# Channel weight pieces in three transfers over 128 partitions, and another order of the decode steps of the token weight pieces

## The chip, the cores and the metric

The kernel runs on one core of one Trainium2 chip, in one launch. A core has five engines with instruction streams of their own: PE multiplies matrices, DVE (VectorE) and ACT (ScalarE) work element by element on 128 partitions, POOL (GpSimd) does small copies and starts some transfers, SP (SyncE) starts the others. Sixteen DMA queues in hardware move the data between HBM and the on-chip memory. The metric is the time of one execution in device microseconds; the lower, the better. Three runs of the kernel before gave 2074.94, 2076.41 and 2078.41 us, so the median is 2076.41.

## The reference

Eight batches of 4096 tokens with 192 values each. First a causal convolution over seven tokens with softmaxed taps, one set of taps for each of eight heads; then a mixing over the tokens, and one over the channels, each with two products, a ReLU between them and a residual.

```python
# w: softmax of weight (8 heads x 7 taps); x_unf: the 7 tokens up to each one
x = np.einsum('hk,bskhg->bshg', w, x_unf).reshape(B, S, D)
xt = x.transpose(0, 2, 1)
h = np.maximum(xt @ w_tok1, 0.0) @ w_tok2          # 4096 -> 256 -> 4096 tokens
u = x + h.transpose(0, 2, 1)
h2 = np.maximum(u @ w_ch1, 0.0) @ w_ch2            # 192 -> 1536 -> 192 channels
return (u + h2).astype(np.float32)
```

The weights come as float64. The kernel reads them as pairs of 32-bit words and makes float32 values of them on the chip ("decoding").

## The kernel before, in words

The batches are worked in five groups (one, one, two, two, two). Within a group the tokens go in tiles of 512: `mix2` adds the token mixing, `transposed` turns the result, `channel1` and `channel2` do the two products of the channel mixing. The convolution and the first token product of the next group run as background beside them. All this takes from about 67 us to the end and is not touched.

What matters here is the opening, `stage1_first`, in which the first batch is convolved on PE (`conv_mm`, with `conv_out` on ACT), the weights are loaded and decoded, and the first token product is summed up (`mix`, L423, into `ps_a`). The work is cut into twelve decode **jobs**, numbered n: jobs 0 to 7 are the eight pieces of `w_tok1` ("token weight pieces", 1024 KB each, results `t_0` to `t_7`), job 8 the first piece of `w_tok2` (1024 KB), jobs 9 to 11 the three **channel pieces** of `w_ch1` (768 KB each). Three pieces of `w_ch2` and a second piece of `w_tok2` follow.

A job goes through these steps, by line:

- L203, `load`: SP issues the transfer into a raw buffer (`dec_raw`, four of them in turn, or `early_raw` for jobs 2, 5 and 8). The issue waits until the buffer's last reader is through, which is L176 of an earlier job.
- L167 on ACT (`begin`): the absolute value, which waits for the landing.
- L169, L170, L173, L176 on DVE, in this order: clamp, shift, sign, low bits. L169 waits for L167. L173 and L176 read the raw buffer again.
- For jobs 8 to 11 also L182 on ACT and L183 on DVE (`split`): the value is split into a high and a low part, `w_hi` and `w_lo` for the channel pieces, `t2s` for `w_tok2`.

Every engine runs its instructions in the order in which they were written, so a waiting instruction holds up all behind it. The order on DVE comes from `woven`, which takes one step from each of its lists in turn: in round n the first two steps of job n, the last two of job n-1, and the split of job n-2. On ACT, L167 of job 11 stands behind the `t2s` split of job 8 and ahead of the first `w_hi` (L182, job 9) and of `h` (L352 in `mix1_done`, the result of the first token product). DVE makes the low half of `h` at L353. `mix2` of the first tile (L844 to L846 on PE) needs `h` and `t2s`, and the first channel products (L919) need `w_hi` and `w_lo`.

SP issues in the order of the program: jobs 8 to 11, the first piece of `w_ch2`, four stores of the convolved batch (`xcd`, L508), then the other two pieces of `w_ch2` and the second piece of `w_tok2`. POOL copies the second tile (`load_next`, L897) when the store of `u` to `xcd` has landed and its buffer is free, and then stores the decoded `w_tok1` (`t1d`, L415) in eight transfers.

A channel piece covers the rows 0 to 191 of `w_ch1` as three blocks c of 64 (`ND` is 3, `D2` is 64), and 256 columns of each of the two column halves h. On the chip the half h = 0 lies on partitions 0 to 63 and h = 1 on partitions 64 to 127. Before, a piece is two transfers, one for each half:

```python
ws = w_ch1.rearrange("(c p) n -> p c n", p=D2)
src = [
    (slice(h * D2, (h + 1) * D2), slice(0, ND * n), ws[:, :, 2 * (h * NP * P + cs.start):2 * (h * NP * P + cs.stop)])
    for h in range(2)
]
```

Of the kernel before, what the change touches and what calls it, by code (L numbers as in the profile page):

```python
# [114 lines left out]
def conv_mixer_kernel(ctx: ExitStack, tc: tile.TileContext, x, weight, w_tok1, w_tok2, w_ch1, w_ch2, out):  # L115
# [6 lines left out]
    P = 128  # L122
# [3 lines left out]
    D2 = P // 2  # L126
    ND = D // D2
    NP = NF // 2
# [12 lines left out]
    w_tok1, w_tok2, w_ch1, w_ch2 = (w.bitcast(U32) for w in (w_tok1, w_tok2, w_ch1, w_ch2))  # L141
# [43 lines left out]
    class Decoder:  # L185
# [5 lines left out]
        def load(self, src, shape, rows=P, raw=None):  # L191

            n = 1
            for s in shape:
                n *= s
            if raw is None:
                raw = self.pool.tile([P, self.n, 2], U32, name="dec_raw", bufs=self.rawbufs)
            flat = raw[:rows, :n]
            for ps, ns, s in (src if isinstance(src, list) else [(slice(0, rows), slice(0, n), src)]):
                d = flat[ps, ns].rearrange("p n t -> p (n t)")  # L200
                if len(s.shape) == 3:
                    d = d.rearrange("p (a b) -> p a b", b=s.shape[2])
                nc.sync.dma_start(out=d, in_=s)  # L203
            return flat, n
# [12 lines left out]
    def w1_job(ps):  # L217

        n = len(ps) * P
        cs = slice(ps.start * P, ps.stop * P)  # L220
        ws = w_ch1.rearrange("(c p) n -> p c n", p=D2)
        src = [
            (slice(h * D2, (h + 1) * D2), slice(0, ND * n), ws[:, :, 2 * (h * NP * P + cs.start):2 * (h * NP * P + cs.stop)])
            for h in range(2)
        ]
        return dict(
            src=src, shape=[ND, n], hi=w1[0][:, :, cs], lo=w1[1][:, :, cs],
            view=lambda v: v.rearrange("p (c n) -> p c n", n=n),
        )
# [30 lines left out]
    def woven(*lists):  # L260

        lists = [list(v) for v in lists]
        while any(lists):
            for v in lists:
                if v:
                    v.pop(0)()

    def decode_items(dec, jobs, loaded=False):
# [35 lines left out]
        def low(i):  # L304
# [7 lines left out]
            items.extend(jobs[i][2])  # L312

        load(0)
        load(1)
        begin(0)
        for i in range(len(jobs)):
            if i:
                high(i - 1)
            for k, c in enumerate((0.5, 0.5, 1, 1)):  # L320
                add(n * c, 500 if k == 0 else 0, lambda i=i, k=k: sts[i]["a"][k]())
                if k == 0 and i:
                    low(i - 1)
                if k == 2:
                    begin(i + 1)
            load(i + 2)
# [35 lines left out]
    def stage1_first(pe, p0, pd, late, load_u, load_next, after, thirds, hooks):  # L362
# [3 lines left out]
        quads = [range(s0, s0 + TJ) for s0 in range(0, NJ, TJ)]  # L366
# [33 lines left out]
        def x0_load(c):  # L400
            x0 = homes[c]
            x0s.append(x0)
            j0 = chunks[c].start
            if c == 0:
                nc.gpsimd.memset(x0[:, 0, :], 0.0)
                nc.sync.dma_start(out=x0[:, 1:], in_=xt[:, 0:NC])
            else:
                nc.sync.dma_start(out=x0, in_=xt[:, j0 - 1:j0 + NC])
# [18 lines left out]

        accs = mix1_accs()
        jobs = [t1_job(i) for i in range(len(quads))] + [t2_job(0, 0, TT)] + [w1_job(ps) for ps in thirds]
        nj = len(jobs)  # L430
        later = [lambda f=f: w2_job(f, NF // 3) for f in range(0, NF, NF // 3)] + [lambda: t2_job(0, TT, TT)]
# [8 lines left out]
        def next_load():  # L440
            n = len(sts)
            if n < nj:
                load(jobs[n])
            else:
                later[n - nj] = later[n - nj]()
                load(later[n - nj])
# [34 lines left out]
        def conv_mm(m):  # L481
            c, part = m // 2, m % 2
            x0 = x0s[c]
            n = NC
            for h2 in range(part * H // 4, (part + 1) * H // 4):
                ps = ps_x.tile([P, TT], F32, name="ps_x")
                convs.setdefault(m, []).append((h2, ps))
                for i in range(2):
                    h = 2 * h2 + i
                    o = ps[:, i * n * G:(i + 1) * n * G].rearrange("p (j g) -> p j g", g=G)  # L490
                    hs = slice(h * G, (h + 1) * G)
                    nc.tensor.matmul(out=o, lhsT=band[:, h], rhs=x0[:, 1:, hs], start=True, stop=False)
                    nc.tensor.matmul(out=o, lhsT=corner[:, h], rhs=x0[:, :n, hs], start=False, stop=True)

        def conv_out(m):
            c, part = m // 2, m % 2
            n = NC
            if c == len(xcs):
                xcs.append(up.tile([P, n, D], F32, name="u", bufs=2))
            xc = xcs[c]  # L500
            for h2, ps in convs[m]:
                nc.scalar.copy(
                    out=xc[:, :n, 2 * h2 * G:2 * (h2 + 1) * G].rearrange("p j (i g) -> p i j g", g=G),
                    in_=ps[:, :2 * n * G].rearrange("p (i j g) -> p i j g", i=2, g=G),
                )

        def xc_store(c):
            nc.sync.dma_start(out=xf[:, chunks[c].start:chunks[c].stop], in_=xcs[c])  # L508

        chains_a = []  # L510

        def begin(n):
            chains_a.append(dec.a(sts[n], jobs[n]["top"]() if "top" in jobs[n] else None))

        def split(n):
            jb = jobs[n]
            hi, lo = jb["make"]() if "make" in jb else (jb["hi"], jb["lo"])
            return dec.b(sts[n], hi, lo, jb.get("view", lambda v: v))
# [23 lines left out]
        for n in range(nj - 1):  # L542
            if n + 2 < nj:
                begin(n + 1)
            if n == 1:
                conv_mm(2)
            for m in behind.get(n, ()):
                conv_out(m)
            woven(
                chains_a[n][:2], chains_a[n - 1][2:] if n else [],  # L550
                split(n - 2) if n > 1 and "top" not in jobs[n - 2] else [],
            )
            if n + 2 == nj:
                begin(n + 1)
            for fn in work.get(n, ()):
                fn()
            if n not in (0, 6, 9):
                next_load()
            if n == 1:
                x0_load(3)  # L560
            if n == 8:
                for c in (3, 0, 1, 2):
                    xc_store(c)
            if n == 7:
                load_u(xcs[0])
            if n == 9:
                late()
        n = nj - 1
# [377 lines left out]
    def channel1(t):  # L946
        h = {}
        for f0 in range(0, NF, NF // 3):
            for n in ("hh", "hl"):
                part = hp.tile([P, NF // 3, TT], F32R, name=f"{n}{f0}")  # L950
                for f in range(NF // 3):
                    h[n, order[f0 + f]] = part[:, f]
        bg.tiled = True
        for p in range(NP):
            pss = channel1_mm(t, p)
            bg.fg(2040 if p else 2400, 1300)
            for f, ps in pss:
                nc.scalar.activation(out=h["hh", f], in_=ps, func=AF.Relu)  # L958
                nc.vector.scalar_tensor_tensor(  # L959
                    out=h["hl", f], in0=ps, scalar=0.0, in1=f32(h["hh", f]), op0=ALU.max, op1=ALU.subtract  # L960
                )
        bg.tiled = False
        return h
# [56 lines left out]
    def first_done():  # L1020
# [6 lines left out]

    thirds = [range(p, p + NP // 3) for p in range(0, NP, NP // 3)]
    stage1_first(
        pe, p0, pd, first_late, first_u, first_next, first_done, thirds,  # L1030
        [first_mix, first_transposed] + [lambda p=p: first_channel1([p]) for p in range(NP)],
# [78 lines left out]
    for gi, bs in enumerate(GROUPS):  # L1110
# [13 lines left out]
        for q in range(NT):  # L1124
            nxt = (gi, q + 1) if q + 1 < NT else (gi + 1, 0)
            for i, b in enumerate(bs):
# [12 lines left out]
                if ahead:  # L1139
                    h = channel1(abc[i])  # L1140
# [67 lines left out]
```

## Time and profile before

| what | value |
|---|---|
| median of three runs | 2076.41 us |
| the profiled execution's own time | 2077.34 us |
| its span in the trace | 2075.5 us |
| PE busy in the span | 2054.5 us |
| DVE busy | 1403.1 us |
| ACT busy | 760.5 us |
| mean granted clock of PE | 0.998 |
| first token mixing (L844) starts at | 58.40 us |
| first channel product (L919) starts at | 67.21 us |

Times in the trace count from the start of the span. A row of the timeline has its start, how long it took, the engine, the line and the operation, then what is written and read, and, in brackets, how long the engine stood idle before it and whose end it waited for. "SPq" is SP issuing a transfer; the transfer itself goes on after it. In the chain of waits a row "DMA ..." is a transfer from its issue to its landing. A stretch's row gives the busy time of PE, PEld (loading weights), DVE, ACT and POOL with their instructions, then the granted clock of PE as a share of the full one, the busy share of the sixteen DMA queues, and the GB/s that they moved.

### The profile page before, as it was taken

The numbers are of one execution on the slowest core, as the hardware profiler recorded it, in microseconds if no ns is written. First come the engines' busy times: TensorE is split into PE (matmuls) and PEld (weight loads), VectorE is DVE, ScalarE is ACT, GpSimd is POOL, SyncE is SP. The second block draws the span as 40 slices with busy tenths as digits, with TensorE's granted clock in tenths as the row PEclk, the third lists the DMA queues.
The fourth block names the chain that finished last, engine by engine and source line by source line (L and its number), as shares of the span: only waits on it lengthen the run. The fifth ranks groups of instructions, "written<-read, shape, count | busy, mean of one in ns | idle before, by whom it ended". The sixth has DMA issues, their size and how long they took to land.

```text
span 2075.5 us, 41299 instructions
## 1 busy us (share of the span) xinstructions
PE 2054.5 (99%) x17723; PEld 1901.4 (92%) x17723; DVE 1403.1 (68%) x2781; ACT 760.5 (37%) x1305; POOL 102.0 (5%) x167
## 2 busy tenths in 40 slices
PE   9899999999999999999999999999999999999999
PEld 9789899998988999999999999999999999999998
DVE  7899969999549989447965678444455544444444
ACT  4565534434333433223333324232232332233222
POOL 0100000000000000000000000000000000000000
PEclk9999999999999999999999999999999999999999
DMA  9745536554363555143543343322211122222210
GB/s 296 284 150 166 162 119 202 157 151 151 117 173 115 168 166 175 60 113 93 150 117 87 105 125 114 103 77 67 59 48 56 50 64 67 59 67 67 67 32 16
DMA packets 259654, 239.44 MB, mean 115 GB/s; under 512 B 202832, under 2 KB 213584, under 8 KB 257936
## 3 DMA queue, kind: packets, MB, share of 16 engines
q1 hardware_dynamic: 243616, 158.55, 26.8%
q0 software_dynamic: 15856, 78.26, 11.8%
q8 instruction: 140, 2.29, 0.4%
q14 instruction: 42, 0.34, 0.0%
HBM read 146.60 MB, written 71.30 MB: 105 GB/s over the span
## 4 chain that ended last, share of the span: by engine, by line
PE 88%; DVE 6%; DMA 3%; ACT 1%; issue 1%; SPq 1%; ACTq 0%
PE ps_x L919 35%; PE ps_x L993 16%; PE ps_x L976 16%; PE ps_x L994 7%; PE ps_x L879 2%; DVE xc L629 2%; PE ps_x L851 2%; PE ps_x L853 2%; PE ps_a L714 2%; PE ps_a L715 2%; PE ps_x L852 2%; PE ps_a L716 2%; DVE hl L959 1%; DMA dec_raw<-in_moe_w_tok_dram 1%; DMA t<-t1d 1%; PE ps_x L848 1%
## 5 line engine op out<-in xcount | busy, mean ns | idle before, releaser
L958 ACT ACTIVATE hh<-ps_x 128x512 fp32r<-128x512 f32 x756 | 411.0, 597 | 807.9 <-PE ps_x L919 807.9
L959 DVE SCALAR_TENSOR_TENSOR hl<-ps_x,hh 128x512 fp32r<-128x512 f32 x756 | 485.0, 685 | 217.6 <-ACT hh L958 216.8
L919 PE MATMUL ps_x<-own,w_hi 64*128 64x512 f32 x2880 | 606.0, 390 | 1.2 <-DVE hl L959 0.9
L993 PE MATMUL ps_x<-w,hh 128*128 128x384 f32 x1872 | 542.9, 361 | 0.2 <-DVE hl L959 0.2
L919 PEld LDWEIGHTS ps_x<-own,w_hi 64*128 64x128 f32 x2880 | 426.2, 184 | 57.8 <-issue 6.5
L994 PE MATMUL ps_x<-w,hl 128*128 128x192 f32 x1872 | 468.7, 250 | 0.0
L919 PE MATMUL ps_x<-other,w_hi 64*128 64x512 f32 x1728 | 451.0, 389 | 0.5 <-DVE osb L998 0.3
L629 DVE SCALAR_TENSOR_TENSOR xc<-raw,cw,xc 128x384 f32<-128x384 f32 (+1 forms) x768 | 388.5, 561 | 9.7 <-ACT xc L627 9.7
L994 PEld LDWEIGHTS ps_x<-w,hl 128*128 128x128 f32 x1872 | 357.5, 191 | 0.0
L993 PEld LDWEIGHTS ps_x<-w,hh 128*128 128x128 f32 x1872 | 351.5, 188 | 0.9 <-DVE hl L959 0.8
L919 PEld LDWEIGHTS ps_x<-other,w_hi 64*128 64x128 f32 x1728 | 314.0, 184 | 33.0 <-DVE hl L959 1.9
L976 PE MATMUL ps_x<-w,hh 64*128 64x384 f32 x2304 | 329.9, 355 | 0.0
L919 PE MATMUL ps_x<-own,w_lo 64*128 64x512 f32 x1440 | 325.3, 386 | 0.0
L976 PE MATMUL ps_x<-w,hl 64*128 64x192 f32 x2304 | 292.1, 247 | 0.1
L919 PE MATMUL ps_x<-other,w_lo 64*128 64x512 f32 x864 | 242.1, 386 | 0.0
L919 PEld LDWEIGHTS ps_x<-own,w_lo 64*128 64x128 f32 x1440 | 216.2, 184 | 25.4
L976 PEld LDWEIGHTS ps_x<-w,hl 64*128 64x128 f32 x2304 | 223.5, 188 | 1.7 <-DVE hl L959 0.8
L976 PEld LDWEIGHTS ps_x<-w,hh 64*128 64x128 f32 x2304 | 219.7, 184 | 0.9
L997 DVE TENSOR_TENSOR osb<-ps_x,u 128x192 f32<-128x192 f32 x156 | 55.4, 355 | 208.1 <-PE ps_x L994 208.0
L919 PEld LDWEIGHTS ps_x<-other,w_lo 64*128 64x128 f32 x864 | 159.0, 184 | 16.4
L881 ACT CAST own<-ps_x 128x512 fp32r<-128x512 f32 x120 | 63.1, 594 | 270.0 <-PE ps_x L879 270.0
L984 DVE TENSOR_TENSOR osb<-ps_x,osb 128x192 f32<-128x192 f32 x288 | 103.0, 358 | 17.4 <-DVE osb L984 0.9
(126 smaller groups left out, 1885.6 us busy)
## 6 DMA issues: line engine op xcount, KB each, us to landing
raw<-in_x_dram SPq DMA_DIRECT2D x56, 672.0 KB, 7.2
t<-t2d SPq DMA_DIRECT2D x64, 512.0 KB, 5.1
out_dram<-osb POOLq DMA_DIRECT2D x63, 384.0 KB, 4.3
u<-xcd SPq DMA_DIRECT2D x62, 384.0 KB, 5.7
xcd<-xc POOLq DMA_DIRECT2D x28, 768.0 KB, 7.1
other<-own POOLq DMA_DIRECT2D x24, 768.0 KB, 5.4
t<-t1p SPq DMA_DIRECT2D x32, 512.0 KB, 4.0
t<-t1d SPq DMA_DIRECT2D x32, 256.0 KB, 4.6
```

What stands on the lines that cost most here:

```text
L629: nc.vector.scalar_tensor_tensor(out=dst, in0=src, scalar=cw[:, h, k:k + 1], in1=dst, op0=ALU.mult, op1=ALU.add)
L714: nc.tensor.matmul(out=ps, lhsT=wh, rhs=xh, start=a, stop=False)
L715: nc.tensor.matmul(out=ps, lhsT=wh, rhs=xl, start=False, stop=False)
L881: nc.scalar.copy(out=own[:, 0, c], in_=ps)
L919: nc.tensor.matmul(out=ps, lhsT=w1[w][rows, c, p * P:(p + 1) * P], rhs=t[h][rows, v, c], start=n == 0, stop=n == len(prods) - 1,)
L958: nc.scalar.activation(out=h["hh", f], in_=ps, func=AF.Relu)
L959: nc.vector.scalar_tensor_tensor(out=h["hl", f], in0=ps, scalar=0.0, in1=f32(h["hh", f]), op0=ALU.max, op1=ALU.subtract)
L976: nc.tensor.matmul(out=ps[:, :m], lhsT=h[part, f][ks, ts], rhs=w2[ks, f, :m], start=n == 0 and part == "hh", stop=z and part == "hl",)
L984: nc.vector.tensor_tensor(out=osb[:, j], in0=v, in1=osb[:, j], op=ALU.add)
L993: nc.tensor.matmul(out=ps[:, :2 * D], lhsT=h["hh", f][:, ts], rhs=w2[:, f, :], start=n == 0, stop=False)
L994: nc.tensor.matmul(out=ps[:, :D], lhsT=h["hl", f][:, ts], rhs=w2[:, f, :D], start=False, stop=z)
L997: nc.vector.tensor_tensor(out=rows(osb[:, j]), in0=rows(ps[:, :D]), in1=tokens(u, i)[:, j], op=ALU.add)
```

## The change

It has two parts. In the first, a channel piece is loaded in three transfers, one for each block c of 64 rows, and each goes to all 128 partitions. The source of such a transfer is walked h, p, n: two halves, 64 rows in each, 512 words in each row. The destination is walked as 128 partitions with 512 words. The other loads keep their shape; the test in `load` is there so that such a three-dimensional source keeps a two-dimensional destination.

In the second, the lists that `woven` takes from are exchanged in rounds 1 to 7: the last two steps of job n-1 come ahead of the first two of job n, one by one in turn. Rounds 8 on stay as they were.

```diff
             for ps, ns, s in (src if isinstance(src, list) else [(slice(0, rows), slice(0, n), src)]):
                 d = flat[ps, ns].rearrange("p n t -> p (n t)")
-                if len(s.shape) == 3:
+                if len(s.shape) == 3 and s.shape[0] == P:
                     d = d.rearrange("p (a b) -> p a b", b=s.shape[2])
                 nc.sync.dma_start(out=d, in_=s)
...
         n = len(ps) * P
         cs = slice(ps.start * P, ps.stop * P)
-        ws = w_ch1.rearrange("(c p) n -> p c n", p=D2)
+        ws = w_ch1.rearrange("(c p) (h n) -> c h p n", p=D2, h=2)
         src = [
-            (slice(h * D2, (h + 1) * D2), slice(0, ND * n), ws[:, :, 2 * (h * NP * P + cs.start):2 * (h * NP * P + cs.stop)])
-            for h in range(2)
+            (slice(0, P), slice(c * n, (c + 1) * n), ws[c, :, :, 2 * cs.start:2 * cs.stop]) for c in range(ND)
         ]
...
+            chains = [chains_a[n][:2], chains_a[n - 1][2:] if n else []]
+
             woven(
-                chains_a[n][:2], chains_a[n - 1][2:] if n else [],
+                *(chains[::-1] if n < len(quads) else chains),
                 split(n - 2) if n > 1 and "top" not in jobs[n - 2] else [],
             )
```

On SP, from job 8 to the stores of the convolved batch, the queue of transfers was this. A row is the line, the destination and source, and the destination's walk; `x6` is six alike in a row. `in_moe_w_ch_dram` stands for both channel weights.

```order
L203 DMA early_raw<-in_moe_w_tok_dram 128x2x1024
L203 DMA dec_raw<-in_moe_w_ch_dram 64x3x512 x6
L203 DMA dec_raw<-in_moe_w_ch_dram 128x4x384
L508 DMA xcd_75<-u 128x1536
L508 DMA xcd_75<-xc_0_122 128x1536
```

And it is now (lines behind the change in `w1_job` stand one lower in the count):

```order
L203 DMA early_raw<-in_moe_w_tok_dram 128x2x1024
L203 DMA dec_raw<-in_moe_w_ch_dram 128x1x512 x9
L203 DMA dec_raw<-in_moe_w_ch_dram 128x4x384
L507 DMA xcd_75<-u 128x1536
L507 DMA xcd_75<-xc_0_122 128x1536
```

Six transfers of three blocks on 64 partitions became nine of one block on 128; what stands ahead and behind is the same. On DVE, rounds 6 and 7 and the start of round 8 (job 8 is the first `dec_top`) were:

```order
L169 TENSOR_SCALAR t_6_131<-t_6_131 128x1024
L173 SCALAR_TENSOR_TENSOR t_5_130<-early_raw,t_5_130 128x1024
L170 TENSOR_SCALAR t_6_131<-t_6_131 128x1024
L176 SCALAR_TENSOR_TENSOR t_5_130<-early_raw,t_5_130 128x1024
L169 TENSOR_SCALAR t_7_132<-t_7_132 128x1024
L173 SCALAR_TENSOR_TENSOR t_6_131<-dec_raw,t_6_131 128x1024
L170 TENSOR_SCALAR t_7_132<-t_7_132 128x1024
L176 SCALAR_TENSOR_TENSOR t_6_131<-dec_raw,t_6_131 128x1024
L169 TENSOR_SCALAR dec_top<-dec_top 128x1024
L173 SCALAR_TENSOR_TENSOR t_7_132<-dec_raw,t_7_132 128x1024
```

The same rounds now:

```order
L173 SCALAR_TENSOR_TENSOR t_5_130<-early_raw,t_5_130 128x1024
L169 TENSOR_SCALAR t_6_131<-t_6_131 128x1024
L176 SCALAR_TENSOR_TENSOR t_5_130<-early_raw,t_5_130 128x1024
L170 TENSOR_SCALAR t_6_131<-t_6_131 128x1024
L173 SCALAR_TENSOR_TENSOR t_6_131<-dec_raw,t_6_131 128x1024
L169 TENSOR_SCALAR t_7_132<-t_7_132 128x1024
L176 SCALAR_TENSOR_TENSOR t_6_131<-dec_raw,t_6_131 128x1024
L170 TENSOR_SCALAR t_7_132<-t_7_132 128x1024
L169 TENSOR_SCALAR dec_top<-dec_top 128x1024
L173 SCALAR_TENSOR_TENSOR t_7_132<-dec_raw,t_7_132 128x1024
```

L173 of a piece moved ahead of L169 of the next; from L169 of `dec_top` on, the order is the old one. PE, ACT and POOL have the same rows as before.

## The prediction

> **What bounds the kernel now.** I read the page first, for the engines' shares; then the stretches with their busy times, to find where PE stands still; then the chain that ended last, in order of time, over the opening; and last the timeline of each engine there, row by row.
>
> ```profile
> PE 2054.5 (99%) x17723; PEld 1901.4 (92%) x17723; DVE 1403.1 (68%) x2781; ACT 760.5 (37%) x1305; POOL 102.0 (5%) x167
> ```
>
> PE is busy for 2054.5 of the 2075.5 us of the span, so only some 21 us are not matmuls, and a change that leaves the matmuls as they are can save little more than that; it can cost any amount. The columns of the next view are the stretch, then each engine's busy time (with instructions), the granted clock of PE, the busy share of the DMA queues and what they moved.
>
> ```profile
> 36.00:38.00 2.00, 2.00 (x14) 2.00 (x14) 2.00 (x3) 0.54 (x2) 0.00 (x0) 1.00 1.01 393
> 38.00:40.00 2.00, 2.00 (x14) 2.00 (x13) 2.00 (x3) 0.00 (x0) 0.00 (x0) 1.00 1.08 227
> 40.00:42.00 2.00, 2.00 (x15) 2.00 (x14) 0.91 (x3) 1.14 (x1) 0.00 (x0) 1.00 1.06 200
> 56.00:58.00 2.00, 0.46 (x3) 0.16 (x1) 2.00 (x3) 1.61 (x2) 0.30 (x1) 1.00 1.04 426
> 58.00:60.80 2.80, 0.35 (x1) 0.19 (x1) 2.77 (x5) 0.85 (x4) 2.80 (x4) 1.00 1.00 417
> 60.80:65.00 4.20, 4.20 (x23) 4.20 (x23) 2.16 (x5) 1.60 (x4) 4.08 (x6) 0.60 1.03 404
> ```
>
> Two things are to be seen. PE has almost nothing to do from 56.5 to 60.8, the longest hole of the run, and works at 0.60 of its clock behind it. And the DMA queues stay fully busy when their rate drops from 393 to 200 GB/s at 38: that is where the transfers of 64 partitions begin. The chain shows what fills the hole:
>
> ```profile
> 30.66 14.81 DMA early_raw<-in_moe_w_tok_dram
> 45.47 0.02 issue
> 45.49 1.15 ACT dec_top L167
> ...
> 60.80 0.36 PE ps_x L845
> ```
>
> The token piece of `w_tok2` (job 8) lands at 45.47, ACT starts on it, and from 46.66 DVE works without a pause until the token mixing of the first tile can start on PE. The rows of ACT, DVE and POOL there (an `x2` row holds two instructions):
>
> ```profile
> 51.22 0.93 ACT L167 ACTIVATE dec_top<-dec_raw 128x768 f32<-128x768 f32 x1 [2.25 <-DMA dec_raw<-in_moe_w_ch_dram]
> 53.47 1.05 ACT L182 CAST t2s<-dec_top 128x1024 fp32r<-128x1024 f32 x1 [1.33 <-DVE dec_top L176]
> 55.95 0.95 ACT L167 ACTIVATE dec_top<-dec_raw 128x768 f32<-128x768 f32 x1 [1.43 <-DVE t2s L183]
> 57.28 0.83 ACT L182 CAST w_hi<-dec_top 128x768 fp32r<-128x768 f32 x1 [0.39 <-DVE dec_top L176]
> 58.02 0.55 ACT L352 ACTIVATE h<-ps_a 128x192 fp32r<-128x192 f32 x2
> 58.15 1.47 DVE L183 TENSOR_TENSOR w_lo<-dec_top,w_hi 128x768 fp32r<-128x768 f32 x1
> 59.54 0.94 DVE L176 SCALAR_TENSOR_TENSOR dec_top<-dec_raw,dec_top 128x768 uint32<-128x768 uint32 x1
> 60.41 0.61 DVE L353 SCALAR_TENSOR_TENSOR h<-ps_a,h 128x192 fp32r<-128x192 f32 x2
> 61.38 0.96 DVE L183 TENSOR_TENSOR w_lo<-dec_top,w_hi 128x768 fp32r<-128x768 f32 x1 [0.36 <-ACT w_hi L182]
> 57.70 1.11 POOL L897 COPY u<-xc 128x768 f32<-128x768 f32 x1 [31.41 <-DMA xcd<-u]
> 58.76 6.12 POOL L415 DMA_DIRECT2D t1d<-t  x8
> ```
>
> The place to remember is ACT at 55.95: that is the Abs of the *third* channel piece. It stands in ACT's order ahead of the first `w_hi` and of `h` (L352), without which L844 to L846 cannot run. Now it waits for DVE alone, since its data are there.
>
> **The change, part one: the loads.** These are the issues in the window 0 to 110 us, with their sizes, and SP's row of the seven that begin with the channel pieces.
>
> ```profile
> 33.22 17.45 SPq L203 DMA_DIRECT2D dec_raw<-in_moe_w_ch_dram  x7
> dec_raw<-in_moe_w_ch_dram SPq DMA_DIRECT2D x6, 384.0 KB, 13.2
> dec_raw<-in_moe_w_ch_dram SPq DMA_DIRECT2D x3, 768.0 KB, 14.1
> t1d<-t POOLq DMA_DIRECT2D x8, 512.0 KB, 11.2
> xcd<-xc SPq DMA_DIRECT2D x3, 768.0 KB, 10.7
> xcd<-u SPq DMA_DIRECT2D x1, 768.0 KB, 6.8
> ```
>
> Six transfers of 384 KB (2304 KB, 2.36 MB) become nine of 256 KB, the same bytes in the same runs of 2 KB. What changes is the walk. Before, both sides of a transfer count 64 partitions outermost. Now the destination counts 128, but the source, `c h p n`, counts *two* halves h outermost and 64 rows inside. No transfer before has such a pair, so its rate must be bounded. From above by the walk with 128 on both sides: 393 GB/s, 6.0 us for all nine. Below that lies the walk of 64 on both sides, 200 GB/s with every queue busy: fewer outer steps cost rate though no queue was idle. From below by a walk whose two outer steps are all that can be dealt out: two of the 16 queues. One queue's rate is 393 / 16 = 24.6 GB/s, with 426 / 16 = 26.6 as the fastest row, so two give 49.1 (53.3), and 2.36 MB take 48.0 us (44.3). I take the low end: a share must be the same bytes on both sides, the two outer counts are 2 and 128, and cutting each along its own outer loop into equal shares works in two, the destination's halves of 64 being just the two h. In all rows seen the outer counts of both sides were equal and multiples of 16, so nothing there speaks for a finer cut.
>
> On such a transfer the Trainium skill has a rule, in "DMA: Bandwidth & Descriptors", section "Why a DMA increments its semaphore by 16 and not by 1": the number of engines is the largest up to 16 that divides the size of the slowest dimension that isn't 1 on both sides. By it 2 and 128 give two engines, hence the same sum; no run so far shows it for a count under 64.
>
> The queues pass from job 8 to the channel pieces at 38 to 39 (227 GB/s lies between 393 and 200). From 38.5 the two queues need 16.0 us for a piece: landings at 54.5, 70.5 and **86.5**. SP issues within the 17 us from 33.22 now; its waits there are for buffers that jobs 3, 4 and 6 leave by 44.77, so the queues, not SP, set these landings. What follows the third landing: Abs 0.95, w_hi 0.83, w_lo 0.96 (the 1.47 ran beside POOL's copy, which will not be there), L176 of the second piece 0.94, the first L353 and PE's start 60.80 - 60.41 = 0.39, and four hand-overs of some 0.03: 4.2 us. All else that DVE did from 50 on is done by then, in the waits for pieces one and two. L845 so starts at 90.7 in place of 60.80: **+29.9 us**, in which PE stands still.
>
> What is late next: everything behind these transfers on the same two queues. They hold a sixteenth each of three `w2` loads, four `xcd` stores, eight `t1d` stores and the second `w_tok2` piece of 1024 KB: 3 x 768 + 4 x 768 + 8 x 512 + 1024 = 10496 KB, 656 KB a queue, 25.3 to 27.3 us. That piece lands at 111.8 to 113.8. Before:
>
> ```profile
> 81.73 1.18 ACT L167 ACTIVATE dec_top<-dec_raw 128x1024 f32<-128x1024 f32 x1
> ...
> 89.28 0.36 PE L849 MATMUL ps_x<-h,t2s 128*128 128x192 f32 x1 [0.74 <-DVE t2s L183]
> ```
>
> 81.73 + 29.9 = 111.6 would leave all as it was; PE already waited 0.74 us at the end of that chain, so a delay there counts in full. It is 0.2 to 2.2; I take **+1.2**. The hole grows from 4 to some 32 us; the half clock behind it (0.60 over 4.2 us) is there already and costs about 1.7 us. I add nothing, with a second such stretch, 1.7, as the upper bound and 0 as the lower.
>
> **Part two: the order on DVE.** For jobs 1 to 7 the last two steps of the job ahead (L173, L176) now lead, so that L173 runs while L169 of the next waits for its data. Two such waits show what it may bring:
>
> ```profile
> 40.04 1.14 ACT L167 ACTIVATE t<-dec_raw 128x1024 f32<-128x1024 f32 x1 [3.50 <-DMA dec_raw<-in_moe_w_tok_dram]
> 41.21 0.69 DVE L169 TENSOR_SCALAR t<-t 128x1024 f32<-128x1024 f32 x1 [1.09 <-ACT t L167]
> 41.82 1.22 DVE L173 SCALAR_TENSOR_TENSOR t<-dec_raw,t 128x1024 uint32<-128x1024 uint32 x1
> 43.55 1.22 DVE L176 SCALAR_TENSOR_TENSOR t<-dec_raw,t 128x1024 uint32<-128x1024 uint32 x1
> 46.66 0.69 DVE L169 TENSOR_SCALAR dec_top<-dec_top 128x1024 f32<-128x1024 f32 x1 [1.89 <-ACT dec_top L167]
> ```
>
> In the wait of 1.09 the step of 1.22 finds room, so DVE is through with job 6 1.09 earlier, at 43.7 instead of 44.77. But the next step is L169 of job 8, whose place does not change, and it waits for a landing. What is won is waited for again there or, with part one as forecast, at the first channel piece until 54.5. Each of the seven L173 now stands directly behind the L170 it needs and loses the overlap that neighbours have (L173 starts 0.61 after L169, which takes 0.69): about 0.1 us each with the hand-over, 0.7 in all, inside DMA waits. I put part two at **0**, between -1.1 and +0.7.
>
> **Sum.** 29.9 + 1.2 + 0 = +31.1 us on the profiled execution's own 2077.34, that is 2108.4. That execution stands 0.9 above the median of the runs shown, 2076.41, so against the median 2107.5; I forecast **2107.5**.
>
> **The rivals.** *The load fills all queues.* If the nine go at 393 GB/s, the half rate is gone: job 8 then lands 2.7 us (1024 KB at 393) behind job 7, whose Abs started on landing at 40.04, so at 42.7; Abs ends at 43.9, and L169 of job 8 starts there (DVE free at 43.7, here part two counts) instead of 46.66: -2.8 us, 2073.6. If the hole on PE, then 1.5 us, no longer brings the half clock, 1.7 more: 2071.9. For it speaks the drop from 393 to 200 with the halves, against it the count of two. The decisive point is whether the nine take less than about 12 us.
>
> The Trainium skill, in "SBUF — State Buffer", section "Door 1: The DMA port swizzle", has it that partitions 0 to 63 reach only 8 of 16 ports and all 128 reach 16; the 393 and 200 agree with it. By it alone this rival would hold.
>
> *The shares are cut along the 64 inner rows.* Then every queue works, but on one half at a time: 200 GB/s, 11.8 us, job 8 lands as now, and the change does not do what it says: 2076.4, within a microsecond. *One queue takes each transfer whole:* 2.36 MB at 24.6 GB/s are 96 us, the third piece lands at 134, 2155.
>
> **How the numbers follow.** Two queues 0.85, all queues 0.08, no change 0.05, one queue 0.02; the first leads because two is the only count that both outer loops allow. Low end: 26.6 GB/s a queue from 38.2, nothing lost behind it: 38.2 + 44.3 + 4.2 - 60.8 = +25.9, 2102. High end: the slowest queue's landing of job 8, 45.47, on one of the two: 45.5 + 48.0 + 4.2 - 60.8 = +36.9, and 2.2 and 1.7 more, +40.8, 2117. Range 2102 to 2118, which holds nearly all of the first case. A difference of 0.2% (4 us) is what a measurement can tell from none. Faster: all queues with the clock, 0.03. Same: the rest of that rival and no change, 0.10. Slower 0.87.
>
> **What would show it.** ACT's L167 on the second and third channel piece waits for the channel DMA some 15 us each time; PE has a hole from 56.5 to about 90; the DMA rate between 46 and 80 is near 50 GB/s with a busy share near 2/16; `xcd` lands after 87. Wrong is the step of two queues if the rate at 38 to 45 stays at 200 or above, and the step behind it if L844 starts before the third piece has landed.

## The result and the profile after

| what | before | after |
|---|---|---|
| median of six runs each, same chip | 2075.55 us (2071.88 to 2078.41) | 2109.34 us (2108.77 to 2110.93) |
| the profiled execution's own time | 2077.34 us | 2109.85 us |
| its span | 2075.5 us | 2108.0 us |
| second product of the first token mixing (L845, now L846) | 60.80 us | 90.95 us |
| second half of the token mixing (L849, now L850) | 89.28 us | 121.19 us |

The ratio is 1.0164, with a 95% interval of 1.0151 to 1.0177: 33.8 us slower, in the forecast range. Lines between the two parts of the change count one lower now, those behind it one higher.

The shares of the engines, and then the stretches, in the same columns as before:

```profile
PE 2058.4 (98%) x17723; PEld 1902.7 (90%) x17723; DVE 1403.9 (67%) x2781; ACT 760.7 (36%) x1305; POOL 101.0 (5%) x167
```

```profile
38.00:40.00 2.00, 2.00 (x14) 2.00 (x13) 1.97 (x3) 1.17 (x1) 0.00 (x0) 1.00 0.29 110
46.00:56.00 10.00, 9.52 (x59) 9.22 (x57) 0.66 (x2) 0.90 (x1) 0.00 (x0) 1.00 0.14 51
60.00:70.00 10.00, 0.00 (x0) 0.00 (x0) 0.00 (x0) 0.00 (x0) 0.00 (x0) 0.51 0.13 49
80.00:88.00 8.00, 0.00 (x0) 0.00 (x0) 0.00 (x0) 0.84 (x2) 0.00 (x0) 0.50 1.04 397
96.00:100.00 4.00, 3.80 (x17) 2.83 (x18) 2.99 (x6) 2.11 (x4) 2.07 (x3) 0.50 1.02 332
```

PE's work is the same (2058.4 us against 2054.5), and what it does not work has grown from 21 to 50 us. From 40 to 77 us the queues are busy for 0.13 to 0.14 of their time, a little over two sixteenths, and move some 50 GB/s; before, the same bytes kept all of them busy at 200. From 60 to 70 no engine does anything at all. The timeline's rows of ACT and PE show who waits for what:

```profile
54.40 0.90 ACT L167 ACTIVATE dec_top<-dec_raw 128x768 f32<-128x768 f32 x1 [8.77 <-DMA dec_raw<-in_moe_w_ch_dram]
70.50 0.89 ACT L167 ACTIVATE dec_top<-dec_raw 128x768 f32<-128x768 f32 x1 [15.19 <-DMA dec_raw<-in_moe_w_ch_dram]
87.16 0.89 ACT L167 ACTIVATE dec_top<-dec_raw 128x768 f32<-128x768 f32 x1 [14.84 <-DMA dec_raw<-in_moe_w_ch_dram]
89.05 0.53 PE L845 MATMUL ps_x<-h,t2s 128*128 128x192 f32 x1 [33.53 <-ACT h L351]
90.95 0.53 PE L846 MATMUL ps_x<-h,t2s 128*128 128x192 f32 x1 [1.37 <-DVE h L352]
121.19 0.36 PE L850 MATMUL ps_x<-h,t2s 128*128 128x192 f32 x1 [0.38 <-DVE t2s L183]
```

Three pieces, three landings, some 16 us apart; behind the third the old chain runs off as it did before, and PE, which had stood still for 33.5 us, goes on. The chain of waits passes through the same place; the issues of channel transfers on SP, the last DMA piece and what follows it:

```profile
50.97 5.22 SPq L203
...
56.30 5.16 SPq L203
...
61.50 5.22 SPq L203
...
66.77 20.29 DMA dec_raw<-in_moe_w_ch_dram
...
87.16 0.89 ACT dec_top L167
88.05 0.73 ACT w_hi L182
...
88.80 0.96 DVE w_lo L183
89.76 0.87 DVE dec_top L176
90.63 0.28 DVE h L352
...
90.95 0.53 PE ps_x L846
```

SP's rows show something that the forecast did not have: each of these issues takes some 5.2 us, the ten issues that begin with the channel pieces take it 45.87 us (7 took 17.45 before), so the first store of `xcd` is issued only at 77.32.

```profile
31.35 45.87 SPq L203 DMA_DIRECT2D dec_raw<-in_moe_w_ch_dram  x10
77.32 1.06 SPq L507 DMA_DIRECT2D xcd<-u  x1
```

### The profile page after: what moved, and what is told of

Same layout as the page of the kernel before. It is cut to its first block, busy times and chain, and to the rows that moved or that the text cites. A ratio compares the mean times of both kernels' runs of the same rounds, so it can differ in the third digit from the quotient of the medians.

```text
span 2108.0 us, 41307 instructions
## 1 busy us (share of the span) xinstructions
PE 2058.4 (98%) x17723; PEld 1902.7 (90%) x17723; DVE 1403.9 (67%) x2781; ACT 760.7 (36%) x1305; POOL 101.0 (5%) x167
## 3 DMA queue, kind: packets, MB, share of 16 engines
q8 instruction: 140, 2.29, 0.4%
## 4 chain that ended last, share of the span: by engine, by line
PE 90%; DVE 4%; DMA 2%; SPq 1%; ACT 1%; issue 0%; ACTq 0%
PE ps_x L920 36%; PE ps_x L994 16%; PE ps_x L977 15%; PE ps_x L995 7%; PE ps_x L880 2%; PE ps_x L852 2%; PE ps_a L715 2%; PE ps_a L716 2%; PE ps_a L717 2%; PE ps_x L854 2%; PE ps_x L853 2%; DVE xc L630 2%; SPq L203 1%; PE ps_x L849 1%; DMA dec_raw<-in_moe_w_ch_dram 1%; DVE hl L960 1%
```

## The experiments

The kernel before ran beside each of them. Its runs spread over some 7 us (2072.48 to 2079.74). Some of that arises in the opening: in the four profiles below that share the old loads on SP and the new order, Abs of job 8 starts anywhere from 42.31 to 43.95. So ratios of many runs decide where a few microseconds matter, and rows of a profile are read against other rows of the same profile.

### The two parts apart

`x_loads_alone` has the new loads with the old order, `x_order_alone` the old loads with the new order.

```diff
-                *(chains[::-1] if n < len(quads) else chains),
+                chains_a[n][:2], chains_a[n - 1][2:] if n else [],
```

> Part one alone: the nine channel transfers of the changed kernel, with the order on DVE of the kernel before. Theory (part one carries all of the change): the same as the changed kernel, 2109 us within 1, with the third channel piece landing near 87 and the PE hole up to about 91. Rival (the new order gives something back or costs something): a difference of 1 us or more from 2109.3.

> Part two alone: the new order on DVE in rounds 1 to 7, with the six half transfers of the kernel before. Theory: L169 of job 8 waits for a landing at 45.5 in either order, so 0, between -1.1 and +0.7 us against 2075.6. Rival (the step that leaves the raw buffer earlier lets SP issue the channel pieces earlier, and DVE is through earlier): 1 to 3 us faster.

Part one alone: 2110.31 us (2109.51 to 2111.53), ratio 1.0168 (1.0154 to 1.0181); its channel pieces' Abs stand at 54.38, 70.48 and 87.07. That is the whole of the change; its interval overlaps the changed kernel's, so the 1 us between the medians is not resolved. Part two alone: 2075.95 us, ratio 0.9999 (0.9991 to 1.0008), no difference to within some 2 us either way. The expectation had job 8 land at 45.5 in either order; in this profile its Abs starts at 42.64. That execution, 2072.60 us, is the fastest of the eleven, so one profile of each order does not tell the share of the order from the spread of the opening.

### What sets the rate: the count of the outer walk

`x_one_stride` walks the source of a transfer as 128 rows of one stride, `x_outer_four` as four blocks of 32. The size, the runs of 2 KB, the destination and the number of transfers are those of the changed kernel. The weights that arrive are not: in `x_one_stride` they come to other partitions, and `x_outer_four` reads the same columns of rows 0 to 95 for all three pieces, so neither computes what the reference does.

```diff
-        ws = w_ch1.rearrange("(c p) (h n) -> c h p n", p=D2, h=2)
+        ws = w_ch1.rearrange("(c p) (h n) -> c (p h) n", p=D2, h=2)     # x_one_stride
+        ws = w_ch1.rearrange("(c p) (h n) -> c h p n", p=D2 // 2, h=4)  # x_outer_four
...
-            (slice(0, P), slice(c * n, (c + 1) * n), ws[c, :, :, 2 * cs.start:2 * cs.stop]) for c in range(ND)
+            (slice(0, P), slice(c * n, (c + 1) * n), ws[c, :, 2 * cs.start:2 * cs.stop]) for c in range(ND)   # x_one_stride
+            (slice(0, P), slice(c * n, (c + 1) * n), ws[c, :, :, 0:2 * n]) for c in range(ND)   # x_outer_four
```

> The changed kernel, with the source of a channel transfer walked as 128 rows of one stride (64 rows and two halves in turn) in place of two halves with 64 rows each; destination, bytes, runs of 2 KB and number of transfers are the same. The weights of the channel product so come to other partitions than the reference has them on. Theory (the outer count of two is what limits the rate): 16 queues work, near 390 GB/s while the channel pieces load, no hole to 91, and 2071 to 2074 us by the forecast's own rival. Rival (the limit lies in the three small transfers, the two-dimensional destination, or SP): about 50 GB/s still, and 2109 us. Between them, were the inner 64 rows what is cut: 200 GB/s and 2076.

> The changed kernel, with the source of a channel transfer walked as four column quarters of 32 rows each, in place of two halves of 64; bytes, runs of 2 KB, destination and number of transfers are the same. Other parts of the channel weights are read than the reference takes. Theory (as many queues as the outer count): four queues, near 100 GB/s, about 8.1 us a piece, third piece landing near 62.7, the second product of the first token mixing (L846) near 67, and about 2082 to 2083 us. Rival (two or more merely falls back to one fixed slow path): as the changed kernel, 50 GB/s and 2109. Rival (any count over two fills the queues): 2071 to 2076.

The stretch from 40 to 44 us in `x_one_stride`, then in `x_outer_four`:

```profile
40.00:44.00 4.00, 4.00 (x26) 4.00 (x25) 3.94 (x6) 2.46 (x4) 0.00 (x0) 1.00 1.03 372
```

```profile
40.00:44.00 4.00, 4.00 (x27) 4.00 (x26) 3.79 (x6) 2.50 (x4) 0.00 (x0) 1.00 0.26 97
```

All queues at 372 GB/s, a quarter of them (0.26) at 97, and with two 0.13 at 49: the busy share follows the outer count, 2, 4 and 128, and the rate follows the share. Destination, size, number and issuer of the transfers are the same, so neither the two-dimensional destination, nor the smaller transfers, nor SP is the limit. All the counts are powers of two, so these runs do not tell the smaller of the two outer counts from the largest number that divides both.

The times: `x_one_stride` 2072.97 us, ratio 0.9984 (0.9976 to 0.9993), which is 2.9 us faster than before and inside the 2071.9 to 2073.6 that the forecast gave its rival of all queues. `x_outer_four` 2086.86 us (ratio 1.0053, 1.0038 to 1.0069), some 4 us over what was expected. Its ACT rows say where some of that is:

```profile
47.01 0.91 ACT L167 ACTIVATE dec_top<-dec_raw 128x768 f32<-128x768 f32 x1 [1.74 <-DMA dec_raw<-in_moe_w_ch_dram]
55.43 0.89 ACT L167 ACTIVATE dec_top<-dec_raw 128x768 f32<-128x768 f32 x1 [7.52 <-DMA dec_raw<-in_moe_w_ch_dram]
64.66 0.89 ACT L167 ACTIVATE dec_top<-dec_raw 128x768 f32<-128x768 f32 x1 [7.41 <-DMA dec_raw<-in_moe_w_ch_dram]
```

The second piece takes 8.4 us, the third 9.2 and not 8.1: at 54.32 SP is through with the channel pieces and issues the stores of `xcd` and two pieces of `w2`, which have their share on the four queues too. That this is what made the third piece later is argued, not shown, and the remaining 2 us of the miss were not followed.

### Behind the hole: the half clock and the backlog

`x_busy` keeps PE at work in the hole; what it computes there is not used.

```diff
         woven(split(n - 1))
+        keep_busy(330)
         hooks[0]()
```

> The changed kernel, with 330 transposes of the identity on PE (L450, some 0.095 us each at the full clock, so 31 us) between the end of the first token product at 55.5 and the first product of the token mixing at 89, while PE would stand still. Theory (the half clock until 101 behind the hole cost some 1.8 us, and the second w_tok2 piece was not late): the second product (L846) starts near 91 as before, the clock is full behind it, the first channel product (L920) starts near 97.3 in place of 99.1, and the time is 1.5 to 2.5 us below the changed kernel's, 2107 to 2108. Rival (the backlog on the two queues costs the 1.2 that the prediction put there): the second w_tok2 piece still ends the wait of PE near 121, and the time stays within 0.5 of 2109.3.

It took 2110.31 us, ratio 1.0165 (1.0151 to 1.0179): nothing won, as the rival had it (the median lies 1.0 above 2109.3, the ratio within 0.0001 of the changed kernel's). The transposes took 36.2 us and not 31, so the first product of the mixing starts behind them, at 90.90. The clock is full, as intended, here from 92 to 96, and the first channel product comes at 95.78, in the changed kernel at 99.12:

```profile
92.00:96.00 4.00, 3.65 (x31) 3.08 (x29) 3.35 (x8) 2.28 (x7) 4.00 (x6) 1.00 0.98 358
```

But the chain of waits behind it now runs through the second `w_tok2` piece, issued at 99.43 and landed at 113.83:

```profile
99.43 14.40 DMA dec_raw<-in_moe_w_tok_dram
...
113.91 1.20 ACT dec_top L167
...
121.47 0.36 PE ps_x L851
```

So two things lie side by side behind the hole, and PE waits for the later. `x_clear` and `x_clear_busy` take the backlog away, without and with PE kept busy (320 transposes in the second):

```diff
         def t1_store(i):
-            nc.gpsimd.dma_start(
+            nc.sync.dma_start(
...
-        for i in range(len(quads)):
-            t1_store(i)
         after()
         hooks[2]()
         woven(chains_a[n][2:])
         next_load()
+        for i in range(len(quads)):
+            t1_store(i)
```

> The changed kernel, with the eight t1d stores (4 MB) issued by SP behind the second w_tok2 piece in place of by POOL ahead of it. The piece then has less ahead of it in the queues and lands before 109 in place of 113.6. Theory (behind the hole two delays lie beside each other, the half clock and the backlog, and either alone holds the end): Abs of this piece comes near 113.7 still, now behind h_first (L932) alone, and the time is within 1 of 2109.3. Rival (the backlog alone is what is lost there): 1.2 to 2 us faster than the changed kernel.

> The same, with 320 transposes on PE in the hole as well, so that both delays are gone. Theory: Abs of the second w_tok2 piece comes 3 to 4 us earlier, near 110, the second half of the mixing (L849, L850) starts near 117.5 in place of 121.2, and the time is 2105 to 2107. Rival (neither of the two is what the end waits for; the reading of t1d or another load takes over): 2109 or more.

The Abs of that piece on ACT, in the changed kernel, `x_loads_alone`, `x_busy`, `x_clear` and `x_clear_busy`, in this order:

```profile
113.66 1.17 ACT L167 ACTIVATE dec_top<-dec_raw 128x1024 f32<-128x1024 f32 x1
```

```profile
113.58 1.14 ACT L167 ACTIVATE dec_top<-dec_raw 128x1024 f32<-128x1024 f32 x1 [0.82 <-DMA dec_raw<-in_moe_w_tok_dram]
```

```profile
113.91 1.19 ACT L167 ACTIVATE dec_top<-dec_raw 128x1024 f32<-128x1024 f32 x1 [0.36 <-DMA dec_raw<-in_moe_w_tok_dram]
```

```profile
111.61 1.17 ACT L167 ACTIVATE dec_top<-dec_raw 128x1024 f32<-128x1024 f32 x1
```

```profile
109.67 1.16 ACT L167 ACTIVATE dec_top<-dec_raw 128x1024 f32<-128x1024 f32 x1
```

In the first three the backlog is there, and the clock from 96 to 100 is 0.50, 1.00 and 1.00 (the row of `x_loads_alone` stands below; that of the changed kernel above): the Abs comes at 113.6 to 113.9 all the same, where the clock is full after a wait for the DMA.

```profile
96.00:100.00 4.00, 3.49 (x26) 2.58 (x27) 3.96 (x7) 1.92 (x4) 1.90 (x3) 1.00 1.01 333
```

In the changed kernel itself the Abs has no wait for the DMA. The chain of waits comes to it from PE, through the first channel products:

```profile
99.19 13.48 PE ps_x L920 x103
112.67 0.94 ACT h_first L932 x2
113.66 1.18 ACT dec_top L167
```

There the first channel product is 99.12 - 67.21 = 31.91 us later than before, and the second half of the mixing is later by the same 31.91. So in this execution all that was lost beyond the hole was lost at the half clock, ahead of any wait for the piece. In `x_loads_alone` the first channel product comes at 97.68, and the chain runs through the DMA piece, issued at 101.33 and landed at 113.50. The two delays end within a microsecond of each other.

That the backlog is one of two queues can be seen too. These are the stretch from 96 to 100 in `x_clear`, where the `t1d` stores come later, and the end of the backlog in the changed kernel:

```profile
96.00:100.00 4.00, 3.49 (x28) 2.57 (x29) 3.60 (x7) 1.92 (x4) 0.00 (x0) 1.00 0.13 49
```

```profile
111.00:112.00 1.00, 1.00 (x12) 0.88 (x10) 0.96 (x3) 1.00 (x3) 0.00 (x0) 1.00 0.12 49
```

Both times the busy share is that of two queues in sixteen (0.13 and 0.12), and the rate 49 GB/s: the others are through.

In `x_clear` and `x_clear_busy` the backlog is gone, no wait for the DMA is left, and the Abs follows PE. The second half of the mixing starts at 119.14 in `x_clear` and 117.20 in `x_clear_busy`, against 121.19. In one point the expectation of `x_clear` was wrong: Abs came 2 us earlier, not at 113.7. The profile gives a reason apart from the edit: its clock was back at 1.00 from 96 to 100, as in `x_loads_alone`, where the changed kernel's had 0.50. How long the half clock lasts behind such a hole is not the same in each execution.

In the end little of this remains: 2109.17 us for `x_clear` (2108.25 to 2109.72) and 2108.25 for `x_clear_busy` (2107.43 to 2109.48), ratios 1.0160 (1.0146 to 1.0174) and 1.0157 (1.0143 to 1.0170). The intervals overlap the changed kernel's, and the 2105 to 2107 expected of `x_clear_busy` was not reached. The row of ACT at 129.38 in `x_clear` shows a place where the 2 us go: the next pieces of `w_tok2` now come late, behind the eight stores that SP issues, and ACT waits 2.29 us for the first of them, where the changed kernel's ACT does not wait for it (at 129.14).

```profile
129.38 0.67 ACT L167 ACTIVATE dec_top<-dec_raw 128x512 f32<-128x512 f32 x1 [2.29 <-DMA dec_raw<-in_moe_w_tok_dram]
```

### The same edits on the kernel before

Each of these has the old loads and the new order (whose cost, if any, was too small to measure): with 40 transposes in the hole from 56.5 to 60.8, with the stores behind, and with both.

> The kernel before with the new order on DVE, and 40 transposes (3.8 us) on PE in the hole from 56.5 to 60.8. Theory (an idle PE brings the half clock in this hole too, worth about 1.7 us): no row below the full clock near 62, 1.2 to 2 us faster than the kernel before. Rival (what PE gains it waits for later at the second w_tok2 piece): within 0.5 us of the kernel before.

> The kernel before with the new order on DVE and the eight t1d stores behind the second w_tok2 piece. Theory: the piece lands near 72 to 75 in place of 79 to 82, the waits of ACT and PE for it go, 0.5 to 1.5 us faster than the kernel before, the rest hidden by the half clock. Rival (the stores on SP hold up what stands behind them, and reading t1d comes late): slower than the kernel before.

> The same, with 40 transposes in the hole from 56 to 60. Theory: with neither the half clock nor the backlog, 2 to 4 us faster than the kernel before, 2072 to 2074. Rival (as in the run with the transposes alone, the gain is lost again): within 1 us of the kernel before.

None is faster: 2076.89 us (ratio 1.0006, 0.9997 to 1.0014), 2076.66 (1.0007, 0.9998 to 1.0016) and 2079.64 (1.0014, 1.0006 to 1.0023). In the first, no half clock is left near 62, but one turns up later. The stretch from 236 to 244 in `x_order_busy`, then in the kernel before:

```profile
236.00:244.00 8.00, 6.07 (x29) 6.07 (x30) 7.62 (x21) 0.80 (x2) 0.00 (x0) 0.79 0.36 105
```

```profile
236.00:244.00 8.00, 6.89 (x47) 6.66 (x46) 7.97 (x22) 0.80 (x2) 0.00 (x0) 1.00 0.45 137
```

The run with both has 0.79 there too, the run with the stores alone and `x_order_alone` 1.00: it is in both profiles with transposes and in none of the three without. Whether the one causes the other was not tried. With the stores alone the wait for the second `w_tok2` piece is gone (Abs at 76.08), but as in `x_clear` ACT waits for the next one, 2.72 us at 94.29. That the run with both is slower than either is not explained.

### Both halves open at a time

The half rate of the kernel before came with 64 partitions. These two keep its transfers and the new order, but let another engine issue the halves for partitions 64 to 127, so that a transfer for each side can be open at a time.

```diff
-                nc.sync.dma_start(out=d, in_=s)
+                (nc.gpsimd if ps.start else nc.sync).dma_start(out=d, in_=s)   # x_halves_pool
+                (nc.scalar if ps.start else nc.sync).dma_start(out=d, in_=s)   # x_halves_act
```

> The kernel before with the new order on DVE, and the half of each channel piece for partitions 64 to 127 issued by POOL in place of SP: six transfers of 64 partitions as before, two of them now open at a time, one for each side. Theory (64 partitions at a time are what halves the rate): near 390 GB/s while the channel pieces load, and 2072 to 2074 us as with one stride. Rival (the two are worked one after the other all the same): 200 GB/s and 2075 to 2076; POOL's copy of the second tile, now behind its third issue, could cost some of it.

> As the run with POOL, with ACT issuing the halves for partitions 64 to 127. Theory: the rate as with POOL, less what ACT loses where its issue waits for a raw buffer ahead of the Abs of jobs 7, 8 and 9: 2072 to 2076. Rival (ACT's waiting issues delay the chain): above 2076.

Both were slower: 2080.01 us (ratio 1.0016, 1.0008 to 1.0025) and 2078.84 (1.0015, 1.0006 to 1.0023). The rate did not come back, here in the run with POOL:

```profile
40.00:44.00 4.00, 4.00 (x27) 4.00 (x26) 2.43 (x3) 1.08 (x1) 0.51 (x1) 1.00 1.05 237
44.00:48.00 4.00, 4.00 (x27) 4.00 (x26) 1.16 (x2) 2.35 (x5) 0.93 (x2) 1.00 1.07 207
```

The queues are full at 237 and 207 GB/s; with ACT these stretches have 256 and 176. So "one side at a time" is not shown to be what halves the rate. It is not excluded either, since the third pair did not start together (POOL issued its half only at 43.49), and no row shows how long two halves were in flight together. Why these runs are slower was not tried, but a place can be seen: POOL issued its first two halves at 30.22 and 33.75, while jobs 7 and 8 were still loading, and Abs of job 8 starts at 45.65 with POOL and 45.74 with ACT, against 42.64 in `x_order_alone`.

## Why the prediction was right

**Two of the sixteen queues.** Right, and shown: two halves outermost give two queues, four blocks give four, 128 rows give all. The forecast had 49.1 GB/s; the stretches show 49 to 51. Of the two rules of the Trainium skill that were weighed, that of "DMA: Bandwidth & Descriptors", section "Why a DMA increments its semaphore by 16 and not by 1", gave two engines, and these traces agree with it at 2, 4 and 128 (shares of 0.13, 0.26 and 1.03). The Trainium skill's "SBUF — State Buffer", section "Door 1: The DMA port swizzle", taken alone gave full rate for a destination of 128 partitions; the 49 GB/s contradict that reading. It holds only once all queues have a share, as in `x_one_stride`.

**The landings.** Forecast 54.5, 70.5 and 86.5; ACT starts on them at 54.40, 70.50 and 87.16. The 48.0 us for the bytes were right to about half a us.

**The 4.2 us behind the third landing, +29.9 on PE.** Measured 90.95 - 60.80 = +30.15. The steps named stand in the chain above, one by one. Two small errors nearly cancel: the piece landed 0.56 later than forecast (66.77 + 20.29 = 87.06), and the steps behind it took 3.89 and not 4.2.

**That SP would not matter.** Half right. The queues set the landings, but SP did not issue "within the 17 us": the ten issues took it 45.87 us, and so 14 queues had nothing to do from 46 to 77 though `w2` and `xcd` were next. These bytes then met the `t1d` stores, issued from 91.87. No run shows what that cost.

**The backlog, +1.2.** The size was about right, but not as this term alone. The late piece is there as forecast: it landed at 113.50 in `x_loads_alone` (issued at 101.33, 12.17 us) and at 113.83 in `x_busy`, in the forecast window of 111.8 to 113.8 or a hair past it, and what is left at the end hangs on about two queues. PE's second half moved by 121.19 - 89.28 = 31.91, which is 1.76 more than the hole. But in the profiled execution these 1.76 are the half clock's, as the chain above shows. The backlog ends a wait only where the clock recovers sooner: in `x_loads_alone` the first channel product is 97.68 - 67.21 = 30.47 late, and the landing makes it 31.81.

**The half clock, 0 added.** The reason given, that it was there already, is not enough: it lasted far longer (0.50 still from 96 to 100), and in the profiled execution it made the whole 1.76. It did not add to the backlog, since the two lie beside each other and end at nearly the same place; `x_busy` took it away and won nothing. The forecast did not see that, and added both terms in its high end. That 1.2 and 0 came so near the sum is in part luck.

**Part two, 0.** Right to within the 2 us that `x_order_alone` resolves. In the changed kernel job 8's L169 came at 42.25, earlier than 46.66, but behind it DVE waited 9.52 us for the first channel piece, as the forecast said.

**The size.** Forecast +31.1, span +32.5: 0.25 from the hole, 0.56 from what lies between it and the second half of the mixing (1.76 for 1.2), and 0.6 that came in behind and was not followed. One place where it may have come in: from 184 to 192 the clock is 0.79 in the changed kernel and 1.00 in the kernel before. The medians lie 33.8 apart, since the profiled execution of before stood 1.8 above its median and that of after 0.5.

## What to carry to other kernels

Look at the outermost counts of both sides of a transfer, not only at how many partitions it fills: a walk that begins with a small count leaves most queues idle, and the profile shows it as a rate that falls together with their busy share (a rate that falls at a full share has another cause). Such a transfer also holds up its issuer, and with it everything behind it. And behind a long hole two delays can lie side by side, so that taking one away shows nothing: take both away before calling either harmless, or laying the loss on one.

## What the runs showed of the hardware that was not expected

- A transfer for two queues holds up its issuer: SP stands some 5.2 us at each of several channel issues, about what two queues at 50 GB/s need for its 262144 bytes.
- The half clock behind a hole of 33.5 us lasted until past 100 us in one execution (0.50 from 96 to 100) and was over by 96 in another of the same opening (1.00 in `x_loads_alone`).
- Half transfers issued by two engines brought 207 to 237 GB/s with POOL and 176 to 256 with ACT, not the 372 of one walk over 128 partitions; how long two of them were in flight together is not shown.
